# Head pairs 2 and 3 of batch 1 by DMA transpose, and paired score steps in batch 0's second half

One Trainium2 chip, one core. The metric is the device time of one execution in microseconds (us); lower is better.

## The reference

Attention with a fixed pattern over 4 batches, 8 heads, 768 tokens, head size 64 (each query sees the first 8 keys and its last 96), then a feed-forward block on all 3072 tokens:

```python
scores = scale * np.matmul(q, k.transpose(0, 1, 3, 2))
keep = is_global | is_local                    # first 8 keys, or 0 <= row - col < 96
scores = np.where(keep, scores - slopes * dist, -1e9)
a = softmax(scores)
x = (a @ v), heads side by side                # 3072 x 512
out = (silu(x @ w_gate) * (x @ w_val)) @ w_out # 512 -> 1536 -> 512
```

## The kernel before

The kernel interleaves the two parts by hand. The feed-forward block goes over eight tiles of 384 tokens; for each 128 columns of the hidden layer there is a gate product and a value product of four matmuls each (`gps`, `vps`), ScalarE makes `th`, VectorE makes `sl` and `hT`; the output products are `ops`. Between these groups stand "steps" of the attention of a later half batch: transposes of q and k (`tr`, `trh`), scores (`sc`, `sch`), values (`va`). A list of stretches says which steps go between which products:

```python
def first(b):                                    # first half of batch b, used for batch 1
    return [[tr(b, 0), tr(b, 1)],
            [sc(b, 0, 0), sc(b, 0, 1)], [sc(b, 1, 0), sc(b, 1, 1)],
            [va(b, 0, 0), tr(b, 2)], [sc(b, 2, 0), sc(b, 2, 1)],
            [va(b, 1, 0), tr(b, 3)], [sc(b, 3, 0), sc(b, 3, 1)],
            [va(b, 2, 0)], [va(b, 3, 0)]]
half1 = [[trh(0)], [trh(1)], [sch(0, 0)], [sch(0, 1)], [trh(2)], [sch(1, 0)], [sch(1, 1)],
         [va(0, 0, 1)], [trh(3)], [sch(2, 0)], [sch(2, 1)], [va(0, 1, 1)],
         [sch(3, 0)], [sch(3, 1)], [va(0, 2, 1)], [va(0, 3, 1)]]   # second half of batch 0
```

For batch 1, q and k come head-major and are transposed on TensorE, 24 matmuls a pair, and copied out by ScalarE and VectorE. Batches 2 and 3 use another way already: rows come token-major, a DMA transposes them, and VectorE spreads the keys into chunks:

```python
def transposes(self):                            # TensorE way
    trq, trk = (t[:, 0:S] for t in banks("trs", FP16))
    for st, tr in ((kst[b], trk), (qst[b], trq)):
        for j in range(J):
            for hi in range(2):
                nc.tensor.transpose(...)
    ...                                          # 3 copies on ScalarE, 1 on VectorE

def transposes_dma(self):                        # DMA way
    for dst, st in ((self.kN, kst[b]), (self.qT, qst[b])):
        nc.sync.dma_start_transpose(out=..., in_=...)

def spread_keys(self):                           # 128x720, 128x48 and 128x56
    nc.vector.tensor_copy(out=k3[:, 0:NCH - 1, NG:], in_=self.kN[:, 0:n]...)
    nc.vector.tensor_copy(out=k3[:, NCH - 1, NG:NG + S - n], in_=self.kN[:, n:S])
    nc.vector.tensor_copy(out=k3[:, :, 0:NG], in_=self.kN[:, 0:NG]...)
```

All attention results go round four banks of PSUM, where TensorE's results land, two a step part (`banks`). In the lines below, `nd` are the two products of a value step (denominators and numerators), `dT`, `dR` and `rb` VectorE's three instructions that invert the denominators, and `xT` the last multiply of a value step, on GpSimd from batch 1 on. A "visit" is one stay of TensorE with the attention between two feed-forward products. A "product" is one group of four feed-forward matmuls.

The softmax here doesn't subtract the row's maximum and nothing guards it: scores larger than these inputs give would overflow.

## Time and profile before

| | before |
|---|---|
| time, median of 4 runs | 260.9 us (260.64 to 261.71) |
| span of the profiled run | 259.1 us |
| TensorE busy | 246.7 us |

How busy each engine is, and where TensorE is idle, stands in the lines that the prediction quotes. For the comparison I cut the span at two marks on TensorE: the q transposes that open batch 0's second half, and batch 1's first transposes; and at the start of batch 1's last value step. Lines of TensorE's timeline of the kernel before (start, us, engine, line, operation, operands, count; in brackets the idle time before it and what ended it):

```profile
27.13 0.36 PE L288 MATMUL trs<-consts,q 128*64 128x128 f16 x6 [0.69 <-DMA q<-in_q_dram]
...
56.26 0.53 PE L262 MATMUL trs<-consts,kst 128*64 128x128 f16 x12
...
78.13 0.45 PE L406 MATMUL nd<-at,ones 128*64 128x216 f16 x8
```

Stretch A, from the first mark to the second, took 56.26 - 27.13 = 29.13 us; stretch B, from the second to the third, 78.13 - 56.26 = 21.87 us.

### The profile page before, as it was taken

To read this page: it belongs to the slowest core of one execution; us is meant where nothing else is said; L and a number is where in the kernel's file an instruction comes from. 1 tells how busy PE (TensorE), PEld (TensorE's weight loads), DVE (VectorE), ACT (ScalarE), POOL (GpSimd) and SP (SyncE) were. 2 spreads that over 40 slices of the span, in tenths; PEclk is the share of its full clock that TensorE was granted. 3 is DMA by queue.
4 is the path that set the end of the run, shared out by engine and by line. 5 is a ranking of instruction groups with operands and counts; after the bars stand their busy time and mean duration, and the time that the engine had idled before them with its cause. 6 is when DMAs were issued, how large, how long until landed. Compare 5 with 4: busy or idle time off the path is not lost.

```text
span 259.1 us, 5560 instructions
## 1 busy us (share of the span) xinstructions
PE 246.7 (95%) x2144; PEld 140.6 (54%) x2144; DVE 184.7 (71%) x423; ACT 133.9 (52%) x296; POOL 100.5 (39%) x117
## 2 busy tenths in 40 slices
PE   7887899899999999899999999999999999999993
PEld 4564455465655566455555566555555566555541
DVE  7378689976786679987876578977875568755510
ACT  3465687559783554465443644664534644332321
POOL 9664762100227919903458767403120232300000
PEclk9999999999999999999999999999999999999999
DMA  6999999990145999994359998955011101101122
GB/s 162 180 201 165 187 204 203 196 60 3 41 62 38 145 162 123 142 167 29 57 72 87 144 171 58 161 83 68 3 40 43 42 3 40 40 3 40 40 83 81
DMA packets 81154, 24.82 MB, mean 96 GB/s; under 512 B 66848, under 2 KB 78184, under 8 KB 81128
## 3 DMA queue, kind: packets, MB, share of 16 engines
q0 software_dynamic: 63264, 13.83, 60.2%
q1 hardware_dynamic: 17720, 10.51, 19.0%
q8 instruction: 17, 0.28, 0.4%
q10 hardware_dynamic: 144, 0.13, 0.2%
q14 instruction: 9, 0.07, 0.1%
HBM read 28.63 MB, written 6.29 MB: 135 GB/s over the span
## 4 chain that ended last, share of the span: by engine, by line
PE 76%; DVE 10%; DMA 8%; POOL 2%; issue 1%; ACT 1%; DVEq 0%; ACTq 0%; POOLq 0%
PE ops L506 23%; PE vps L477 22%; PE gps L477 20%; PE nd L406 6%; DMA q<-in_q_dram 5%; DMA k<-in_k_dram 3%; PE sc L358 3%; DVE sl L490 2%; DVE dT L422 2%; DVE rb L427 1%; DVE hT L494 1%; PE trs L262 1%; DVE xT L434 1%; DVE kT L457 1%; DVE dR L423 1%
## 5 line engine op out<-in xcount | busy, mean ns | idle before, releaser
L488 ACT ACTIVATE th<-gps 128x384 f32<-128x384 f32 x94 | 46.5, 494 | 76.9 <-PE gps L477 76.2
L490 DVE SCALAR_TENSOR_TENSOR sl<-th,gps 128x384 f32<-128x384 f32 x94 | 51.6, 549 | 38.0 <-ACT th L488 37.2
L477 PE MATMUL vps<-xT,wv 128*128 128x384 f16 x376 | 76.8, 327 | 1.5 <-DVE sl L490 1.4
L477 PE MATMUL gps<-xT,wg 128*128 128x384 f16 x376 | 76.6, 326 | 0.1
L506 PE MATMUL ops<-wo,hT 128*128 128x512 f16 x288 | 75.4, 379 | 0.0
L434 POOL TENSOR_TENSOR xT<-ns,rb 128x384 f16<-128x384 f32 x24 | 24.0, 1002 | 91.0 <-DVE rb L427 54.5
L494 DVE TENSOR_TENSOR hT<-vps,sl 128x384 f16<-128x384 f32 x94 | 51.1, 544 | 6.9 <-PE vps L477 2.0
L477 PEld LDWEIGHTS <-wg 128*128 128x128 f16 x384 | 36.5, 98 | 34.4 <-issue 2.1
L477 PEld LDWEIGHTS <-wv 128*128 128x128 f16 x384 | 34.7, 98 | 26.4 <-issue 4.2
L506 PEld LDWEIGHTS <-hT 128*128 128x128 f16 x288 | 27.7, 98 | 25.3 <-issue 0.5
L367 ACT ACTIVATE at<-sc 128x432 f16<-128x432 f32 x72 | 32.9, 538 | 1.5 <-PE sc L358 1.5
L171 POOL DMA_DIRECT2D vS<-in_v_dram x25 | 22.3, 895 | 7.6 <-DMA wo<-in_moe_w_out_dram 4.9
L520 ACT ACTIVATE osb<-ops 128x512 f32<-128x512 f32 x23 | 13.9, 604 | 15.6 <-PE ops L506 15.6
L419 ACT COPY ns<-nd 128x384 f32<-128x384 f32 x28 | 13.4, 479 | 9.9 <-PE nd L406 7.8
L427 DVE STREAM_TRANSPOSE rb<-dR 128x384 f32<-128x384 f32 x32 | 18.0, 566 | 0.4
L422 DVE STREAM_TRANSPOSE dT<-nd 128x384 f32<-128x384 f32 x28 | 16.0, 570 | 0.0
L378 DVE TENSOR_TENSOR at<-at,masks 128x864 f16<-128x864 f16 x20 | 14.3, 714 | 2.1 <-ACT at L367 1.6
L343 ACT ACTIVATE at<-sc 128x432 f16<-128x432 f32 (+2 forms) x32 | 11.9, 443 | 5.8 <-PE sc L335 5.8
L406 PEld LDWEIGHTS <-ones 128*64 128x64 f16 x288 | 10.9, 110 | 7.0 <-issue 6.6
L196 POOL DMA_DIRECT2D kst<-in_k_dram x16 | 13.7, 866 | 0.0
L196 POOL DMA_DIRECT2D qst<-in_q_dram x16 | 13.6, 868 | 0.0
L406 PE MATMUL nd<-at,ones 128*64 128x216 f16 (+6 forms) x256 | 13.2, 230 | 0.0
(79 smaller groups left out, 192.7 us busy)
## 6 DMA issues: line engine op xcount, KB each, us to landing
out_dram<-osb SPq DMA_DIRECT2D x23, 256.0 KB, 2.0
vS<-in_v_dram POOLq DMA_DIRECT2D x21, 120.0 KB, 6.5
wg<-in_moe_w_gate_dram POOLq DMA_DIRECT2D x6, 256.0 KB, 8.4
wv<-in_moe_w_val_dram POOLq DMA_DIRECT2D x6, 256.0 KB, 8.8
wo<-in_moe_w_out_dram POOLq DMA_DIRECT2D x3, 512.0 KB, 12.0
kst<-in_k_dram POOLq DMA_DIRECT2D x16, 96.0 KB, 4.1
qst<-in_q_dram POOLq DMA_DIRECT2D x16, 96.0 KB, 4.3
kst<-in_k_dram POOLq DMA_DIRECT2D x2, 384.0 KB, 15.5
```

Of the source, the lines that this page charges most:

```text
L171: nc.gpsimd.dma_start(out=vSs[b][NG:NG + n, c, :, :], in_=v[b, :, KC * c:KC * c + n, :].rearrange("h p d -> p h d"))
L196: nc.gpsimd.dma_start(out=st[:, h // 2, :, h % 2, :], in_=src[b, h].rearrange("(t p) d -> p t d", p=128))
L367: nc.scalar.activation(out=at[:, hi, :], in_=sc[hi][:, 0:BANK], func=AF.Exp, scale=scale)
L406: nc.tensor.matmul(dst[r, o:o + n], lhsT=ones[:, 0:64] if ones_side else vals[:, 2 * hp + hi, :], rhs=self.at[cb][:, hi, col:col + n], sta ...
L422: nc.vector.transpose(dT, den[:, 0:TB])
L427: nc.vector.transpose(rb.rearrange("p (n i) -> p n i", i=32), dR.unsqueeze(2).broadcast_to([128, TB // 32, 32]))
L434: mul_eng.tensor_mul(dst, src, rb)
L477: nc.tensor.matmul(gv[f, which][:, 0:TB], lhsT=w[:, c, 128 * f:128 * f + 128], rhs=x_of(t)[:, c, :], start=(c == 0), stop=(c == NC - 1))
L488: nc.scalar.activation(out=th, in_=dst[:, 0:TB], func=AF.Tanh, scale=0.5)
L490: nc.vector.scalar_tensor_tensor(out=sl, in0=th, scalar=1.0, in1=dst[:, 0:TB], op0=AluOp.add, op1=AluOp.mult)
L494: nc.vector.tensor_mul(hTs[t][:, f, :], dst[:, 0:TB], gv["sl"])
L506: nc.tensor.matmul(ops, lhsT=hTs[t][:, f, 128 * i:128 * i + 128], rhs=wo[:, f, :], start=(f == 0), stop=(f == NFF - 1))
```

## The change

Its intent: take half of batch 1's transposes off the engine that is full, get their rows in time by moving V's loads, and interrupt the feed-forward products less often. The core of the diff (the views on the shared buffer are cut):

```diff
     def first(b):
         return [[tr(b, 0), tr(b, 1)],
-                [sc(b, 0, 0), sc(b, 0, 1)], [sc(b, 1, 0), sc(b, 1, 1)],
-                [va(b, 0, 0), tr(b, 2)], [sc(b, 2, 0), sc(b, 2, 1)],
-                [va(b, 1, 0), tr(b, 3)], [sc(b, 3, 0), sc(b, 3, 1)],
-                [va(b, 2, 0)], [va(b, 3, 0)]]
+                [sc(b, 0, 0), sc(b, 0, 1)], [sc(b, 1, 0), sc(b, 1, 1), fetch(b, 2, 3)],
+                [va(b, 0, 0)], [sp(b, 2), va(b, 1, 0), sp(b, 3)],
+                [sc(b, 2, 0), sc(b, 2, 1)],
+                [sc(b, 3, 0), sc(b, 3, 1)], [va(b, 2, 0)], [va(b, 3, 0)]]
-    half1 = [[trh(0)], [trh(1)], [sch(0, 0)], [sch(0, 1)], [trh(2)], [sch(1, 0)], [sch(1, 1)],
-             [va(0, 0, 1)], [trh(3)], [sch(2, 0)], [sch(2, 1)], [va(0, 1, 1)],
-             [sch(3, 0)], [sch(3, 1)], [va(0, 2, 1)], [va(0, 3, 1)]]
+    half1 = [[trh(0)], [trh(1)], [sch(0, 0), sch(0, 1)], [trh(2)], [sch(1, 0), sch(1, 1)],
+             [va(0, 0, 1), trh(3)], [sch(2, 0), sch(2, 1)], [va(0, 1, 1)],
+             [sch(3, 0), sch(3, 1)], [va(0, 2, 1)], [va(0, 3, 1)]]
...
-    at_step(0, 9, lambda: load_qk(1, 4, 8))
     for c in range(4):
-        at_step(0 if c < 2 else 1, (10 + c) % 12, lambda c=c: load_v_rest(1, c))
+        at_step(0, 8 + c, lambda c=c: load_v_rest(1, c))
+    for n in range(8):
+        at_step(*((0, 9 + n // 2) if n < 6 else (1, 0)),
+                lambda hp=2 + n // 4, i=1 - n // 2 % 2, e=n % 2: load_rows(1, i, 2 * hp + e))
```

`fetch` issues the DMA transposes, `sp` queues the spreading copies for VectorE.

More of the change, by code (lines that the diff above doesn't have):

```diff
@@ L192, in stage_rows, with rows_of @@
         kst[b] = sb2.tile([128, NP, J, 2, D], FP16, name="kst", tag="kst")
+    def rows_of(st, b, hp):
+        if b > 1:
+            return st[b][:, hp]
+        return st[b][:, 2 * hp:2 * hp + 2, :].rearrange("p h x -> p (h x)").rearrange(
+            "p (t e d) -> p t e d", t=J, e=2)
     def load_rows(b, i, h):
-        st, src = ((qst[b], q), (kst[b], k))[i]
+        st, src = ((qst, q), (kst, k))[i]
         nc.gpsimd.dma_start(
-            out=st[:, h // 2, :, h % 2, :],
+            out=rows_of(st, b, h // 2)[:, :, h % 2, :],
             in_=src[b, h].rearrange("(t p) d -> p t d", p=128))
@@ L444, in transposes_dma @@
             self.kN = sb2.tile([128, S], FP16, name="kN", tag="kN", bufs=2)
-            for dst, st in ((self.kN, kst[b]), (self.qT, qst[b])):
+            for dst, st in ((self.kN, kst), (self.qT, qst)):
                 nc.sync.dma_start_transpose(
                     out=dst.rearrange("r (t p) -> r t p", t=J),
-                    in_=st[:, hp].rearrange("p t e d -> p (t e d)"))
+                    in_=rows_of(st, b, hp).rearrange("p t e d -> p (t e d)"))
         def spread_keys(self):
@@ L657, in second, with fetch, sp @@
                 [va(b, 0, 1), va(b, 1, 1)], [va(b, 2, 1), va(b, 3, 1)]]
+    def fetch(b, *hps):
+        return lambda: [pairs[b, hp].transposes_dma() for hp in hps]
+    def sp(b, hp):
+        return lambda: later.append(pairs[b, hp].spread_keys)
     def first(b):
         return [[tr(b, 0), tr(b, 1)],
-                [sc(b, 0, 0), sc(b, 0, 1)], [sc(b, 1, 0), sc(b, 1, 1)],
-                [va(b, 0, 0), tr(b, 2)], [sc(b, 2, 0), sc(b, 2, 1)],
-                [va(b, 1, 0), tr(b, 3)], [sc(b, 3, 0), sc(b, 3, 1)],
-                [va(b, 2, 0)], [va(b, 3, 0)]]
+                [sc(b, 0, 0), sc(b, 0, 1)], [sc(b, 1, 0), sc(b, 1, 1), fetch(b, 2, 3)],
+                [va(b, 0, 0)], [sp(b, 2), va(b, 1, 0), sp(b, 3)],
+                [sc(b, 2, 0), sc(b, 2, 1)],
+                [sc(b, 3, 0), sc(b, 3, 1)], [va(b, 2, 0)], [va(b, 3, 0)]]
     def both(b):
         n = b + 1
-        def fetch(*hps):
-            return lambda: [pairs[n, hp].transposes_dma() for hp in hps]
-        def sp(hp):
-            return lambda: later.append(pairs[n, hp].spread_keys)
-        return [[sc(b, 0, 2), sc(b, 1, 2)], [sc(b, 2, 2), sc(b, 3, 2), fetch(0, 1)],
-                [va(b, 0, 1), va(b, 1, 1)], [sp(0), va(b, 2, 1), va(b, 3, 1), sp(1)],
-                [sc(n, 0, 0), sc(n, 0, 1), fetch(2, 3)], [sp(2), sc(n, 1, 0), sc(n, 1, 1)],
-                [va(n, 0, 0), sc(n, 2, 0)], [sp(3), sc(n, 2, 1), va(n, 1, 0)],
+        return [[sc(b, 0, 2), sc(b, 1, 2)], [sc(b, 2, 2), sc(b, 3, 2), fetch(n, 0, 1)],
+                [va(b, 0, 1), va(b, 1, 1)], [sp(n, 0), va(b, 2, 1), va(b, 3, 1), sp(n, 1)],
+                [sc(n, 0, 0), sc(n, 0, 1), fetch(n, 2, 3)], [sp(n, 2), sc(n, 1, 0), sc(n, 1, 1)],
+                [va(n, 0, 0), sc(n, 2, 0)], [sp(n, 3), sc(n, 2, 1), va(n, 1, 0)],
                 [sc(n, 3, 0), sc(n, 3, 1)], [va(n, 2, 0)], [va(n, 3, 0)]]
-    half1 = [[trh(0)], [trh(1)], [sch(0, 0)], [sch(0, 1)], [trh(2)], [sch(1, 0)], [sch(1, 1)],
-             [va(0, 0, 1)], [trh(3)], [sch(2, 0)], [sch(2, 1)], [va(0, 1, 1)],
-             [sch(3, 0)], [sch(3, 1)], [va(0, 2, 1)], [va(0, 3, 1)]]
+    half1 = [[trh(0)], [trh(1)], [sch(0, 0), sch(0, 1)], [trh(2)], [sch(1, 0), sch(1, 1)],
+             [va(0, 0, 1), trh(3)], [sch(2, 0), sch(2, 1)], [va(0, 1, 1)],
+             [sch(3, 0), sch(3, 1)], [va(0, 2, 1)], [va(0, 3, 1)]]
     def ff(t, f0, f1, n_out=(0,)):
```

## The prediction

> **What bounds the kernel now.** I read the page's engine shares first, then the busy time of each engine in stretches, then the matmul order and TensorE's waits in the two stretches that the change touches. The shares:
>
> ```profile
> PE 246.7 (95%) x2144; PEld 140.6 (54%) x2144; DVE 184.7 (71%) x423; ACT 133.9 (52%) x296; POOL 100.5 (39%) x117
> ```
>
> TensorE is busy 246.7 of 259.1 us, so only work taken off it, or some of its 12.4 us of idle time, can shorten the kernel. The windows tell where the idle time lies (each row: stretch, then its length, then PE, PEld, DVE, ACT, POOL busy):
>
> ```profile
> 26.00:37.00 11.00, 10.31 (x129) 5.88 (x128) 8.01 (x22) 8.39 (x21) 7.27 (x11) 1.00 1.55 193
> 37.00:53.30 16.30, 14.77 (x153) 8.50 (x148) 15.30 (x35) 10.32 (x28) 3.85 (x5) 1.00 1.43 197
> 53.30:56.30 3.00, 3.00 (x21) 1.59 (x21) 2.29 (x6) 1.25 (x3) 0.00 (x0) 1.00 0.87 55
> 56.30:81.50 25.20, 25.20 (x288) 14.92 (x288) 19.24 (x45) 19.43 (x42) 5.83 (x7) 1.00 0.24 33
> ```
>
> From 26 to 53 us (batch 0's second half, mixed with the first feed-forward tile) TensorE loses 0.69 + 1.53 = 2.2 us, and VectorE is nearly full from 37 on (15.30 of 16.30). From 56 to 81 us (batch 1's first half) TensorE never stops, and VectorE and ScalarE have about 6 us each to spare. What TensorE waited for from 24 to 56 us:
>
> ```profile
> PE vps L477 <- DVE sl L490: 0.7, 1, 0.7
> PE trs L288 <- DMA q<-in_q_dram: 0.7, 1, 0.7
> PE sc L335 <- DVE kT L301: 0.6, 1, 0.6
> ```
>
> The third is not for data but for a bank: four score banks go round, and the second score step of a pair gets the two that the transposes just filled, which VectorE has yet to copy out.
>
> **What the skill says.** (1) "TensorEngine Tiling (Array Packing)", Key Properties: changing the tiling mode drains TensorE. The trace agrees; pieces of the chain, in order of time (start, us, what):
>
> ```profile
> 64.25 0.66 PE nd L406 x16
> 64.92 0.69 PE trs L262 x24
> 65.60 0.76 PE gps L477 x4
> 66.36 0.65 PE vps L477 x4
> ```
>
> Four feed-forward matmuls take 0.65 us, and 0.76 after 64-wide work: 0.11 us for each visit to the attention. (2) "VectorE: DVE Perf Modes", The three transpose paths: a 128x128 transpose takes 390 ns on TensorE and 1309 ns by the DMA crossbar. Here 24 half-width ones in a row take 0.69 us, 29 ns each; a DMA transpose of 768 tokens lands 6.3 to 6.4 us after its issue. So the DMA way pays by moving work off the full engine, not by being quick. (3) "DMA: Bandwidth & Descriptors", Why small descriptors are slow: a fixed cost per packet. The trace agrees (two stretches of 2 us with the queue full, the first moving 768-byte packets, the second 128-byte ones):
>
> ```profile
> DMA packets 546, 0.41 MB, mean 203 GB/s; under 512 B 18, under 2 KB 546, under 8 KB 546
> DMA packets 2204, 0.29 MB, mean 147 GB/s; under 512 B 2140, under 2 KB 2204, under 8 KB 2204
> ```
>
> (4) "SBUF — State Buffer", SBUF: two separate sides: VectorE copies of this sort and GpSimd lock each other out. The small kT copy from kN, 0.17 us alone, indeed took 0.99 us at 101 us:
>
> ```profile
> 100.82 0.71 DVE L454 COPY kT<-kN 128x720 f16<-128x720 f16 x1
> 101.46 0.99 DVE L457 COPY kT<-kN 128x48 f16<-128x48 f16 x1
> 102.36 0.17 DVE L458 COPY kT<-kN 128x56 f16<-128x56 f16 x1
> ```
>
> **The change, part by part.**
>
> *Transposes of pairs 2 and 3.* The built program has 2096 matmuls instead of 2144: 48 transposes go, which are two of the 0.69 us pieces shown: 1.38 us. They lie where TensorE is never idle, so all of it should show. They were done in the same visit as a value step, so no visit is saved there. ScalarE also loses two sets of copies (0.77 + 0.22 + 0.83 = 1.8 us each), and VectorE two of 0.18 us; it gains two sets of three spreading copies, 0.7 us (0.34 + 0.17 + 0.17) undisturbed to 1.9 us (as at 101 us), so 1 to 3.4 us net, against 6 us spare. Neither is on the path.
>
> *Rows and DMA.* Two loads of 384 KB (512 packets of 768 bytes, at 273 a us: 1.9 us each, 3.8) become eight of 96 KB (768 packets of 128 bytes, at 1100 a us: 0.7 us each, 5.6). In the kernel before the load queue stays full until 55 to 56 us; it will now run dry near 58. V chunks now stand among and ahead of the rows, but the queue is full either way, so their place only decides which rows come last. Each load waits in the program for the one eight before it, and the issue costs 0.87 us on GpSimd, which has nothing else to do until its first multiply at 68.5 us. The four transposes stand first in SP's program, before any output store, and wait only for rows and for a qT buffer free since about 44 us; so they start when rows land, not when the step comes. SP needs about 1.3 us for each issue. Estimate: rows of pair 2 by 53 to 55 us, kN of pair 2 by 61, the last qT by 65 to 66. They are wanted later: the fifth step of the stretch, ahead of which VectorE meets the first spreading copy, stands near 66 us (steps were at 56.3, 59.8, 62.3, 64.2 and 67.6 before; the new fifth is a value step with one transpose set less ahead of it), and the first score step of pair 2 near 68. A margin of some 5 us for pair 2, and 2 to 3 for pair 3. Nothing of it should reach TensorE.
>
> *Pairing.* Sixteen steps become eleven. The order of TensorE's instructions in the built programs shows five fewer visits: 5 x 0.11 = 0.55 us less. The first transposes also come one product (0.65 us) later, which covers the 0.69 us wait for q: about 0.65 us less. Against this, with both score steps at once all four banks are in use, and between the filling of a bank and its next use there is now often one product (0.76 us) where there were two. Emptying takes two exponentials (0.95 us) or the kT copies (0.68 us) behind a sl or hT of 0.55 us, so five or so places may wait 0.2 to 0.5 us each; I put 0.9 us. And VectorE cannot go faster than its work: of 27.3 us from 26 to 53.3 it has 23.3, so 4.0 us of slack is the most that this stretch can ever give. Net: 0.55 + 0.65 - 0.9 = 0.3 us less.
>
> **Sum.** 1.38 + 0.3 = 1.7 us less: 260.8 - 1.7 = 259.1 us.
>
> **The rivals.**
> *Pairing makes new bank waits.* For it: the 0.6 us wait for L301 is just of this kind with two products between, and VectorE is full; a masking multiply queued behind four exponentials holds up the copies behind it. Against it: ScalarE is only 60 to 75% busy there, and there are more products between steps on average. If each of six places waited 0.5 us, the 3 us would eat the 1.2 us of gains and the transposes: 261.2 us.
> *Rows come late.* For it: 6144 more small packets at the end of a full queue, and DMA transposes beside them. In the kernel before, q0 and the transposes of batch 2 ran together from 88 to 98 us at 155 GB/s without stopping TensorE for more than 0.7 us. If it happened, VectorE would sit in front of a spreading copy and hold up every sl behind it: 2 to 6 us, 262 to 265 us.
> *Pairing clears the stretch.* Fewer visits and the late start remove most of the 2.2 us idle time and no wait takes its place: 1.38 + 0.55 + 2.0 = 3.9 us, 256.9 us. Against it: the 15.30 of 16.30.
> *Transposes were hidden anyway.* Then only the pairing counts: 260.5 us. Against it: no idle time in 56 to 81 us.
>
> **Range and chances.** The 1.38 us I hold near certain; pairing lies between -1.5 and +1.8 us around its -0.3; lateness adds a tail upwards. So 257.7 to 261.0 us. Faster by 2% needs 255.6 us, 5.2 us less, more than idle time, transposes and visits concerned together (2.2 + 1.38 + 0.55 = 4.1): 2%. Slower by 2% needs 266.0 us, which only late rows give: 3%.
>
> **What would show it.** Right: 48 matmuls of L262, none waited for; the stretch from batch 1's first transposes to its last value step about 1.4 us shorter with TensorE full; no TensorE or VectorE wait for kN or the row loads; DMA dry by 58 to 59 us; the stretch before it within 1.5 us of its old length, with waits of sc, trs or nd for ACT or DVE under 0.6 us each. Wrong: idle time of VectorE before the spreading copies, a gap of TensorE near 66 to 70 us, or bank waits of 2 us and more in 27 to 52 us.

## More of the kernel before

In all timelines read here VectorE's instructions start in the order of the program.

A wait for q falls ahead of the mark and is not in A.

## The result, and the profile after

259.06 us median of 4 runs (259.04 to 259.59), against 260.9 us: ratio 0.9929, 95% interval 0.9903 to 0.9955, so within 2%, and 1.84 us less. Ratios here are the mean time of one kernel's fast runs over the mean of the other's of the same rounds, so not quite the ratio of the medians. The number predicted was 259.1 us. That does not yet say that its terms were right. The three marks in the kernel after:

```profile
27.68 0.33 PE L295 MATMUL trs<-consts,q 128*64 128x128 f16 x6
...
55.69 0.53 PE L269 MATMUL trs<-consts,kst 128*64 128x128 f16 x12
...
77.08 0.45 PE L413 MATMUL nd<-at,ones 128*64 128x216 f16 x8
```

Stretch A is 28.01 us, 1.12 us less; stretch B is 21.39 us, 0.48 us less. The first mark came 0.55 us later in this profiled run, and the part after the third mark took 180.72 instead of 180.97 us: 0.55 - 1.12 - 0.48 - 0.25 = -1.3 us, the difference of the spans (257.8 and 259.1). So the transposes gave a third of the predicted 1.38 us. Pairing gave more than the predicted 0.3 us in A, but 0.65 of the 1.12 us is the product that now stands ahead of the mark; what that is worth in time, e1 to e3 tell.

TensorE's waits from 24 to 56 us (engine, line, what it waited for: us in total, times, longest):

```profile
PE gvps L484 <- DVE xT L441: 1.2, 1, 1.2
PE vps L484 <- DVE sl L497: 0.7, 1, 0.7
PE sc L342 <- DVE kT L308: 0.6, 1, 0.6
PE sc L331 <- DVE dT L429: 0.5, 1, 0.5
```

The first stands ahead of stretch A, in both kernels. The wait for q is gone, and one for a value bank (`dT` empties it) has come. In stretch B, where TensorE had not waited at all, the chain that ended last now leaves it for 4 us. The chain from 66 to 73 us (start, us, what):

```profile
66.39 0.66 PE nd L413 x16
67.05 0.77 PE gps L484 x4
...
67.84 0.50 ACT th L495
...
68.37 0.55 DVE sl L497
68.92 0.51 DVE dT L429
...
69.45 0.23 DVE dR L430
69.68 0.41 DVE hT L501
70.09 0.48 DVE rb L434
70.58 0.23 DVE kT L461
70.80 0.09 DVE kT L464
70.89 0.90 DVE kT L465
...
71.84 0.54 PE sc L365 x8
```

From `sl` to the last of pair 3's spreading copies VectorE has no pause, and the scores of pair 3 start when it is done. TensorE's timeline of scores 2 and scores 3:

```profile
69.04 0.78 PE L365 MATMUL sc<-qT,kT 64*128 64x216 f16 x8
...
71.84 0.54 PE L365 MATMUL sc<-qT,kT 64*128 64x216 f16 x8 [0.62 <-DVE kT L465]
```

The last copy took 0.98 us instead of 0.17, and a GpSimd multiply started just ahead of it (VectorE's and GpSimd's timelines):

```profile
70.80 0.98 DVE L465 COPY kT<-kN 128x56 f16<-128x56 f16 x1
```

```profile
70.73 1.01 POOL L441 TENSOR_TENSOR xT<-ns,rb 128x384 f16<-128x384 f32 x1 [1.95 <-DVE rb L434]
```

The Trainium skill, "SBUF — State Buffer", SBUF: two separate sides, says that a VectorE instruction of certain kinds and a GpSimd instruction lock each other out of a pair of ports that they share, for a whole instruction; the trace agrees, as the multiply ended at 71.74 us and the copy at 71.78. Pair 2's 128x720 copy met the multiply before it in the same way (0.98 us from 67.06 on, instead of 0.34), but VectorE was idle for 0.15 us after that set of copies.

Late rows are not the reason. The DMA queue of SP:

```profile
52.41 1.32 SPq L453 DMA_TRANSPOSE kN<-kst  x1
54.60 1.21 SPq L453 DMA_TRANSPOSE qT<-qst  x1
57.39 1.21 SPq L453 DMA_TRANSPOSE kN<-kst  x1
59.18 1.21 SPq L453 DMA_TRANSPOSE qT<-qst  x1
```

Each starts when its rows have landed, the DMA rate falls to nothing by 62 us, and the first spreading copy runs at 67.06 us with no idle time of VectorE before it.

**Noise.** Medians of one kernel moved by 0.5 us and single runs by over 1 us. Much of it arises before the first mark. The ten filler matmuls near 6.5 us took 1.26 or 1.27 us in seven of the twelve profiles and 2.06 to 2.31 us in five. The Trainium skill, "TensorE: Matmul & The Clock Gate", What's actually happening, tells of a clock that is released after some 3.4 us of activity, counted in a free-running window; these two durations (a ratio of 1.8) would fit that, but the view of granted clock shows 1.00 there in both cases, and no run here shows that this is the cause. So I judge by the stretches, which repeat to 0.04 us where the steps concerned are alike, and use times as the check on the whole.

### The profile page after: what moved, and what is told of

Read it like the earlier page. It is cut to its first block, busy times and chain, and to the rows that moved or that the text cites. A ratio compares the mean times of both kernels' runs of the same rounds, so it can differ in the third digit from the quotient of the medians.

```text
span 257.8 us, 5484 instructions
## 1 busy us (share of the span) xinstructions
PE 246.1 (95%) x2096; PEld 140.5 (54%) x2096; DVE 185.0 (72%) x427; ACT 131.1 (51%) x290; POOL 105.8 (41%) x123
## 4 chain that ended last, share of the span: by engine, by line
PE 78%; DVE 13%; ACT 4%; issue 2%; DMA 1%; SPq 0%; DVEq 0%; ACTq 0%
PE ops L513 23%; PE vps L484 21%; PE gps L484 20%; PE nd L413 6%; PE sc L365 3%; DVE sl L497 2%; DVE dT L429 2%; ACT at L350 2%; DVE rb L434 2%; DVE hT L501 2%; DMA q<-in_q_dram 1%; PE warm L541 1%; PE psv L565 1%; DVE xT L441 1%; DVE dR L430 1%
## 5 line engine op out<-in xcount | busy, mean ns | idle before, releaser
L203 POOL DMA_DIRECT2D qst<-in_q_dram x20 | 16.9, 858 | 2.7 <-DMA wo<-in_moe_w_out_dram 1.6
L203 POOL DMA_DIRECT2D kst<-in_k_dram x20 | 17.0, 860 | 2.1 <-DMA wo<-in_moe_w_out_dram 1.7
L385 DVE TENSOR_TENSOR at<-at,masks 128x864 f16<-128x864 f16 x20 | 13.2, 661 | 1.9 <-ACT at L374 1.6
```

The lines of the kernel that those rows point to most:

```text
L203: nc.gpsimd.dma_start(out=rows_of(st, b, h // 2)[:, :, h % 2, :], in_=src[b, h].rearrange("(t p) d -> p t d", p=128))
```

## The experiments

Theory at the start: the result is the sum of a pairing part and a transposing part; the first is larger than predicted, the second smaller because of the copies on VectorE. Rivals: the prediction's own sizes; pairing does nothing since VectorE sets the pace; the transposes had been hidden.

| kernel | A, us | B, us | median us (runs) | ratio to before, 95% interval |
|---|---|---|---|---|
| before | 29.13 | 21.87 | 260.9 (4) | |
| after | 28.01 | 21.39 | 259.06 (4) | 0.9929 (0.9903 to 0.9955) |
| e1 pairing alone | 28.00 | 21.87 | 259.93 (6) | 0.9968 (0.9944 to 0.9992) |
| e2 rows alone | 29.10 | 21.39 | 260.33 (6) | 0.999 (0.9971 to 1.001) |
| e3 paired, begun earlier | 28.72 | 21.39 | 259.78 (6) | 0.9972 (0.995 to 0.9993) |
| e4 copies of pair 3 earlier | 28.01 | 22.22 | 260.29 (6) | 0.999 (0.9958 to 1.0023) |
| e5 all copies two steps earlier | 28.02 | 21.12 | 259.34 (6) | 0.9947 (0.9916 to 0.9979) |
| e6 extra bank | 27.11 | 21.38 | 258.16 (1) | |
| e7 transposes twice | 29.14 | 23.19 | 261.13 (1) | |
| e8 V last | 27.99 | 21.39 | 259.23 (1) | |
| e9 e5 with the old step order | 27.98 | 20.48 | 258.4 (6) | 0.9901 (0.9867 to 0.9936) |
| e10 e9 and e6 | 27.08 | 20.48 | 257.39 (6) | 0.9874 (0.9847 to 0.9901) |

All gave correct results.

### e1, e2: each part alone

e1 is the kernel before with the new `half1`; e2 is the kernel after with the old one.

```diff
-    half1 = [[trh(0)], [trh(1)], [sch(0, 0)], [sch(0, 1)], ...]   # 16 steps
+    half1 = [[trh(0)], [trh(1)], [sch(0, 0), sch(0, 1)], ...]     # 11 steps; e2 the reverse
```

> The kernel before with only the paired steps of batch 0's second half (eleven steps instead of sixteen); transposes, loads and their times as before. Theory A (the result is the sum of two parts, and pairing gives more than the 0.3 us predicted): five visits less (0.55 us) plus one product done while q is still landing (0.65 us) less about 0.5 us of new bank waits, so 0.7 to 1.3 us less than before, ratio 0.995 to 0.997, and no TensorE wait for q. Rival B (the prediction's own sizes): 0.3 us less, ratio 0.999. Rival C (pairing gives nothing, VectorE sets the pace from 37 to 53 us): no change within 0.15 us.

> The changed kernel with the sixteen unpaired steps put back: rows, DMA transposes and V loads alone. Theory A: 1.38 us of transposes go, about 0.6 us comes back as one TensorE wait for a spreading copy that ran beside a GpSimd multiply, so 0.6 to 0.9 us less than before, ratio 0.9965 to 0.9977; e1 and e2 together make up the whole. Rival B (prediction): 1.38 us less, ratio 0.9947, no such wait. Rival C (the transposes were hidden): under 0.2 us.

Each part moves its own stretch by what the whole change moves it, to 0.03 us, and leaves the other stretch alone. Theory A's split into two parts holds. The rows give 0.48 us in B rather than 1.38, less than the 0.6 to 0.9 us that Theory A had for them. By time e1 is 0.8 us faster; e2's 0.3 us can't be told from nothing by its interval, only by its stretch. (The two times add up to 1.1 us of the 1.84; the intervals are too wide to say more.) In e1 I had written that the wait for q would vanish; it shrank to 0.42 us, as q landed near 27.5 us in that run.

What pairing is worth in time is seen from a product that stands ahead of the mark in all of these kernels, the first `gps` after TensorE's wait for `xT`. In e1 it starts at 25.34 us, as in the kernel before, and batch 1's transposes start at 55.51 instead of 56.26: 0.75 us. Where nobody waits for q the same distance is 30.04 us without pairing (e2) and 29.60 with it (the kernel after): 0.44 us. So pairing is worth more than the prediction's 0.3 us, though less than A's 1.13.

### e3: paired steps begun one product earlier

```diff
-        owed = -0.1 if n == 0 else 0.4
+        owed = 0.15 if n == 0 else 0.4
```

> The changed kernel with the paired steps begun one product earlier, so that the first transposes of batch 0's second half stand where they stood before the change. Theory A: the wait for q comes back, 0.4 to 0.7 us slower than the changed kernel (ratio to before 0.994 to 0.996). Rival: the wait for q never set the end, VectorE does: the same as the changed kernel within 0.2 us (ratio about 0.993).

Counted from the q transposes, A is 28.72 us, 0.71 more than the kernel after: the one product that no longer runs ahead of them. But in this run TensorE came to that point 0.55 us later than in the profile of before and found q landed, so it paid no wait. So both texts miss a point: the later start is worth up to 0.7 us when TensorE gets there before q, and nothing when its own start was late. Of the 1.12 us of pairing some 0.7 is of this kind, and 28.72 against 29.13, that is 0.41 us, is sure; the 0.44 us between e2 and the kernel after says the same. The edit shifted some later steps too (a wait of 1.02 us for `hT` stands in place of the 0.69 for `sl`), so it is no pure test of the start. The times (0.9972, against 0.9929) can't settle it, as their intervals overlap.

### e4: copies of pair 3 ahead of the value step

```diff
-                [va(b, 0, 0)], [sp(b, 2), va(b, 1, 0), sp(b, 3)],
+                [va(b, 0, 0)], [sp(b, 2), sp(b, 3), va(b, 1, 0)],
```

> The changed kernel with the spreading copies of pair 3 put ahead of pair 1's value step instead of after it, so that they run before the GpSimd multiply of that value step starts. Theory A (two engines locked out of each other make the 0.62 us wait of the scores of pair 3): the 128x56 copy takes 0.17 us instead of 0.98, the TensorE wait for it goes, 0.4 to 0.7 us less than the changed kernel, ratio to before about 0.991. Rival (the copy waits for the DMA transposes): VectorE sits idle before the copies now and the time is the same or longer.

The copies of pair 3 now take 0.34, 0.17 and 0.17 us, as Theory A had it, and still stretch B grew, by 0.83 us. VectorE's and TensorE's timelines of e4:

```profile
67.38 0.34 DVE L461 COPY kT<-kN 128x720 f16<-128x720 f16 x1
...
67.80 0.54 DVE L501 TENSOR_TENSOR hT<-vps,sl 128x384 f16<-128x384 f32 x1
68.27 0.57 DVE L429 STREAM_TRANSPOSE dT<-nd 128x384 f32<-128x384 f32 x1
```

```profile
67.58 0.45 PE L365 MATMUL sc<-qT,kT 64*128 64x216 f16 x5
68.89 0.34 PE L365 MATMUL sc<-qT,kT 64*128 64x216 f16 x3 [0.86 <-DVE dT L429]
```

The second half of scores 2 needs the banks of the value step, and `dT`, which empties one of them, stands behind six copies in VectorE's order. Scores 3 of this run also lost 0.64 us (70.57 to the next product at 71.69, where 0.48 is usual), with ScalarE as the releaser; e5 explains this. So the lock-out lengthens a copy (0.98 against 0.17 us), but as the whole cause it falls. What costs is that the copies stand in VectorE's queue between two score steps at all; which wait they cause depends on the place.

### e5: copies where VectorE has time

```diff
-        return [[tr(b, 0), tr(b, 1)],
-                [sc(b, 0, 0), sc(b, 0, 1)], [sc(b, 1, 0), sc(b, 1, 1), fetch(b, 2, 3)],
-                [va(b, 0, 0)], [sp(b, 2), va(b, 1, 0), sp(b, 3)],
+        return [[tr(b, 0), tr(b, 1), fetch(b, 2, 3)],
+                [sc(b, 0, 0), sc(b, 0, 1), sp(b, 2)], [sc(b, 1, 0), sc(b, 1, 1), sp(b, 3)],
+                [va(b, 0, 0)], [va(b, 1, 0)],
```

> The changed kernel with the DMA transposes asked for one step earlier and the spreading copies of pairs 2 and 3 put behind the score steps of pairs 0 and 1, where no GpSimd multiply runs and VectorE still has idle time. Theory A (the copies cost TensorE time through VectorE's order: as the changed kernel has them they run beside a multiply and hold up the scores, one step earlier they hold up the emptying of the value banks): all waits of TensorE from 57 to 80 us go, and the stretch from batch 1's first transposes to its last value step falls from 21.39 us to 20.5 us, the full 1.38 us below the 21.87 of the kernel before. Rival (the DMA transposes have not landed that early): VectorE sits idle before the copies and TensorE waits at the scores of pair 1 or the values; the stretch is 21.4 us or more.

All six copies took 0.34 and 0.17 us, VectorE did not wait for them, and no TensorE wait for VectorE is left in B. Yet B fell only to 21.12 us. The rest is a wait of another engine, in TensorE's and ScalarE's timelines of e5:

```profile
70.70 0.67 PE L365 MATMUL sc<-qT,kT 64*128 64x216 f16 x5
71.54 0.34 PE L365 MATMUL sc<-qT,kT 64*128 64x216 f16 x3 [0.17 <-ACT at L374]
```

```profile
70.54 2.64 ACT L374 ACTIVATE at<-sc 128x432 f16<-128x432 f32 x6
```

Scores 3 occupied 1.11 us (70.70 to the next product at 71.81) where an undisturbed step takes 0.48: 0.63 us lost, of which the view calls only 0.17 idle. Its second half needs the banks of scores 2, and the exponentials that empty them are put off until just before this step, then run six in a row. In the kernel before a value step and a set of transposes stood between scores 2 and 3; the change put the two next to each other. Theory A and its rival were both wrong about what would be left.

### e6: a fifth bank for the key transposes

```diff
-            pairs[0, hp].transposes_half(1, [t[:, 0:TB] for t in banks("trs", FP16)], V)
+            if hp < 2:
+                trs = banks("trs", FP16)
+            else:
+                trs = [single("trs", state["tags"][state["n"] % 4], FP16), single("trs", "o0", FP16)]
+                state["n"] += 1
+            pairs[0, hp].transposes_half(1, [t[:, 0:TB] for t in trs], V)
```

> The changed kernel with the key transposes of pairs 2 and 3 of batch 0's second half in a fifth bank that is idle there, so that the second score step of a pair does not wait for VectorE's key copies. Theory A (the waits for banks are real losses): the 0.6 us wait of the scores for the key copies goes and the stretch from the second-half gate products to batch 1's first transposes falls from 31.85 us to 31.2 to 31.4. Rival B (VectorE's work sets the pace): the wait goes, the wait of the products for sl near 49 us grows by about as much, and the stretch stays within 0.15 us of 31.85.

(I gave stretch A there from the last gate products, 31.85 us in the kernel after; it fell to 31.21.) From 24 to 56 us TensorE's waits after the first are now

```profile
PE vps L484 <- DVE sl L497: 0.6, 1, 0.6
PE sc L342 <- DVE dT L429: 0.5, 1, 0.5
```

The wait for the key copies is gone, that for `sl` has not grown, and A is 0.90 us shorter. The bank waits are real losses; VectorE, though 93% busy from 37 to 53.3 us in the kernel after (15.20 of 16.30 us), does not set the pace. (From the last gate products the gain is 0.64 us: 0.26 us more went between the k and q transposes, ahead of the mark. The view names no releaser there; a wait for q is likely and not shown.)

### e7: what the transposes cost by themselves

The kernel before, with the transposes of pairs 2 and 3 done twice into the same banks:

```diff
-                for j in range(J):
+                for j in [j for j in range(J)] * (2 if b == 1 and hp > 1 else 1):
```

> The kernel before with the TensorE transposes of pairs 2 and 3 of batch 1 done twice into the same banks, same result: 48 matmuls more. If a transpose costs TensorE its 29 ns in full, the stretch from batch 1's first transposes to its last value step grows from 21.87 to 23.25 us, 1.38 more. If part of it is hidden under waits for VectorE or ScalarE, it grows by less, down to nothing.

B grew by 1.32 us for 48 matmuls, 27.5 ns each. They lie fully on the path; the rival that they were hidden falls.

### e8: the place of V

```diff
-    for c in range(4):
-        at_step(0, 8 + c, lambda c=c: load_v_rest(1, c))
     for n in range(8):
         ...                                     # the rows
+    for c in range(4):
+        at_step(1, 0, lambda c=c: load_v_rest(1, c))
```

> The changed kernel with V's first four chunks of batch 1 loaded after the q/k rows instead of between and ahead of them. Both ways the queue runs dry near 58 to 60 us and V is wanted at 63.6 us: no stretch changes by more than 0.1 us (21.39 us from batch 1's first transposes to its last value step), the DMA transposes start 2 to 4 us earlier. Rival (the place of V matters): TensorE waits for V at its first value step of batch 1.

No stretch moved by more than 0.02 us. The transposes started at 50.57, 52.09, 53.44 and 55.52 us, 1.8 to 4.0 us earlier. V's place cost and gained nothing.

### e9, e10: the two losses taken out

e9 is e5 with scores 2 back between the first two value steps; e10 adds e6's edit.

```diff
-                [va(b, 0, 0)], [va(b, 1, 0)],
-                [sc(b, 2, 0), sc(b, 2, 1)],
+                [va(b, 0, 0)], [sc(b, 2, 0), sc(b, 2, 1)],
+                [va(b, 1, 0)],
```

> The spreading copies as early as in the fifth run, and the score step of pair 2 put back between the first two value steps, as the kernel before has it (first values, scores 2, second values, scores 3). In the fifth run the second half of scores 3 lost 0.64 us: it waited for banks that ScalarE emptied only 1.2 us before, because scores 2 and 3 follow each other without a value step between. Theory A (the change's new order of steps costs that, once the copies are out of the way): the wait goes, the stretch from batch 1's first transposes to its last value step falls from 21.12 us to 20.4 to 20.6, the full 1.38 us below the kernel before. Rival (another wait takes its place, for the value banks or for VectorE's masks): 21.0 us or more.

> The ninth run's order with the sixth run's extra bank as well. If the two losses are in separate stretches they add: 0.9 us less than the changed kernel in each, 1.8 us together, ratio to before about 0.986 (some 257 us), both stretches at their best values (27.1 us from the q transposes to batch 1's first transposes, 20.4 to 20.6 us after). Rival: the time saved is lost again in the later batches, which are paced by something else, and the whole gains less than 1 us on the changed kernel.

TensorE's timeline of e9:

```profile
66.22 0.54 PE L365 MATMUL sc<-qT,kT 64*128 64x216 f16 x8
...
68.75 0.45 PE L413 MATMUL nd<-at,ones 128*64 128x216 f16 x8
...
70.82 0.54 PE L365 MATMUL sc<-qT,kT 64*128 64x216 f16 x8
```

Both score steps run unbroken, and no wait is left in B: 20.48 us, 1.39 less than before, which is the 1.38 us of the prediction. In e10 both stretches are at their best, and the part after the third mark is as in the kernel after (180.76 and 180.72 us), so nothing was lost again later. e10 took 257.39 us, ratio 0.9874, 3.3 us less on average than the kernel before in the same rounds (0.0126 of some 260.5 us), the fastest of all tried. Its stretches are together 0.93 + 0.91 = 1.84 us shorter than those of the kernel after; the times of the two, from different calls, differ by 1.67 us.

## Why the prediction was right or wrong

That the time came out to 0.1 us was luck. The transposing term was too large by 0.90 us, the pairing term too small, a quarter of a microsecond at the end was not forecast at all, and the interval of the ratio allows 1.2 to 2.5 us less. (The sum also starts from 260.8 us, 0.1 below the median.) Of the prediction's own signs, the 1.4 us shorter stretch B with TensorE full failed, and its sign of being wrong, a gap of TensorE near 66 to 70 us, came true a little later, at 71.2 us.

- **"Transposes ... 1.38 us: all of it should show."** The cost was right (e7: 1.32 us; e9: 1.39 us), what showed was 0.48 us. The step that failed is "Neither is on the path", said of the copies on ScalarE and VectorE. I had counted 6 us spare on VectorE over 25 us, an average; the change puts six copies between two score steps, where VectorE runs without a pause for 3.4 us, from `sl` on. Two losses stand there together: scores 2 last 0.71 us (69.04 to the next product at 69.75) instead of 0.48, scores 3 start some 0.69 us late. 0.23 + 0.69 = 0.92 us is 1.38 - 0.48 to 0.02 us. And with those copies gone a third cause stood behind them (e5): scores 2 and 3 next to each other wait for ScalarE. I had read the new list of steps for visits, not for the distance between users of one bank.
- **Rows and DMA: right.** Nobody waited for them. The rows of pair 2 had landed by 52.4 and 54.6 us, as estimated; the last rows by 59.2 us; the last transpose landed near 62 us, not 65 to 66, so the margin was larger than told. The rival of late rows falls.
- **Pairing: the direction right, the size too small.** Predicted 0.3 us; measured 0.44 to 0.75 us in time, by whether q is waited for, and 1.12 us in A. Two terms are mis-sized. The 0.9 us for new bank waits was too much: they were 0.61 us for the key copies, in place of 0.58, and 0.45 us for `dT`, together 0.48 us more. That they are of the kind described, e6 shows. And the 0.55 us for five visits was too little. By the distances from start to start in TensorE's timelines, and without its waits (1.30 us before, 1.75 after), A spends 19.59 and then 18.42 us on products and 8.24 and then 7.84 us on attention steps. With 0.65 us off for the product that moved, that is 0.52 + 0.40 = 0.92 us for five visits, 0.18 us each. A product takes 0.75 us ahead of a visit and 0.65 otherwise, and the attention steps became shorter as well where they were joined; the prediction's 0.11 us counted about the first of the two. 0.65 + 0.92 - 0.45 = 1.12 us is the whole of A. The late start covers the wait for q only so far as TensorE is there first (e1, e3). The rival that VectorE's fullness sets the pace there falls with it.
- **Transposes hidden anyway: wrong** (e7).
- **Left open:** the part after the third mark is 180.72 to 180.77 us in all nine kernels with the eight row loads and 180.97 to 181.03 in the three without (the spans are given to 0.1 us). Most of the quarter of a microsecond lies after VectorE's last instruction has begun (3.22 against 3.44 us to the end of the span). No run was made to find out why.

## What to carry to other kernels

Work moved off a full engine lands in another engine's order: look at what stands in that queue between the instructions that the full engine waits for, not at the average of free time. When steps are regrouped, write down for each bank how many products lie between its filling and its next use; here one extra bank (e6) and, in e9, copies placed earlier with one swap of two steps shortened the two stretches by 1.84 us more, as much again as the whole change. When a prediction hits, check its terms by stretches before believing it.

## What the Trainium skill lacked or had wrong

- "VectorE: DVE Perf Modes", The three transpose paths, gives one duration for a 128x128 transpose on TensorE, and the page of TensorE adds another; neither gives the cost of transposes in a row, which decides here: 48 half-width ones cost 1.32 us, 27.5 ns each.
- "TensorEngine Tiling (Array Packing)", Key Properties, says that a change of mode drains TensorE, without a size; here a visit to the attention, which changes it on the way in and out, cost 0.18 us.
- "TensorE: Matmul & The Clock Gate", What's actually happening, describes a slow start of this sort; no page tells whether a granted clock as the profile gives it would show it. Here it read 1.00 while ten fillers took 1.27 us in some runs and 2.31 in others.
